# Attention, spatial gating and token mixing on one core: the order of all engines through the mixing stages comes from a list scheduler in the kernel

## The chip, the core and the metric

The kernel runs on one NeuronCore of a Trainium2 chip. Its engines work side by side, each through its own list of instructions in order: TensorE (PE, matrix products into PSUM), VectorE (DVE), ScalarE (ACT), GpSimd (POOL) and SyncE (SP), which here only issues transfers between DRAM and the on-chip memory. They wait for each other through semaphores. The metric is the device time of one execution in microseconds, the median of the runs shown; lower is better.

## The reference

Three computations follow one another; B = 4, H = 8 heads of D = 48, S = 768 positions, so that H x D = 384 columns.

```python
f = 1.0 / (1.0 + np.exp(-f_logit))
for t in range(S):                                   # gated linear attention
    state = f[:, :, t, :, None] * state + np.einsum('bhd,bhe->bhde', k[:, :, t], v[:, :, t])
    y[:, :, t] = np.einsum('bhd,bhde->bhe', q[:, :, t], state)
...
h = np.maximum(x @ w_in, 0.0)                        # spatial gating: d_ff = 1024
u, v = (h[..., :d_ff // 2], h[..., d_ff // 2:])
v_n = (v - mu) / np.sqrt(var + 1e-06)
v_s = np.einsum('ts,bsd->btd', w_spatial, v_n) + b_spatial[None, :, None]
x = (u * v_s) @ w_out
...
h = np.maximum(x.transpose(0, 2, 1) @ w_tok1, 0.0) @ w_tok2    # token mixing: 256
u = x + h.transpose(0, 2, 1)
return u + np.maximum(u @ w_ch1, 0.0) @ w_ch2                  # feed-forward: 1536
```

Most weights arrive as 64-bit floats, viewed as pairs of 32-bit words; w_spatial (w_sp) arrives as 32-bit floats.

## The kernel before

All products are made of a high and a low part (`mm3`: high x high, high x low, low x high), so every operand is first split: a rounded copy (high) and the rest (low).

**Attention.** The work is cut into 32 units: 4 batches x 2 halves of the sequence (384 positions) x 4 pairs of heads. A unit (`att_unit`, with `chunked`) loads fkq (keys, queries and decay logits of the pair), takes a sigmoid on ACT, two running products on VectorE (`tensor_tensor_scan`), scales keys and queries, then on TensorE transposes the keys and forms the pairs (`pt`, `pa`), on ACT copies them, on GpSimd masks them (`am`), on TensorE sums keys by values (`pk`), on VectorE carries the state from chunk to chunk, and on TensorE forms `py`, the sum of what the state and the masked pairs give. ACT and VectorE take the high and the low part of `py` into the tile x of that half. The fourth pair does not fit in its place: six small transfers scatter its rows over the other pairs' tiles. PSUM holds one `pt`, one `pk`, one `py` and one set of `pa`; there are three fkq buffers.

**Mixing stages.** For each batch and half, `s1` makes three `norm` tiles (nine products of 512 columns, Relu, mean and variance, scaled, split into vh and vl) and four `gate` tiles (nine products of 384 columns, Relu). `s23` makes four `mix` tiles for each half (18 products over all six tiles of vh and vl of the batch and the split w_sp; the bias added, times the gate, split again) and three `out1` tiles (twelve products with w_out; to DRAM as x1d). Their PSUM tiles come from a pool of three. A batch is 28 such tiles.

**Weights.** `split_weight` loads a piece of 384 columns into a staging buffer (`wst`, three of them, for 64-bit weights; `wsa`, three, for what is rounded). For 64-bit weights `rounded` makes a 32-bit float of the two words: two VectorE passes, an ACT scaling, a GpSimd addition. An ACT copy gives the high part; the low part is the difference, made for w_in, w_sp and w_out by two products on TensorE (the piece times the identity, minus the high part) and an ACT eviction. w_t1, w_t2 and w_c1 are rounded early, in 22 pieces, and stored to DRAM; they are loaded and split again in the last mixing stage, with a GpSimd subtraction.

**What sets the order.** The beginning, up to the first half's attention units, is written in a fixed turn (`apart`, `weave`) and then ordered by the framework's scheduler. From there on TensorE's order is as written: `run` walks through the mixing tiles and at set places (`turns`, counted in tiles) lets `keys` and `sums` take an attention unit one step further. The order of VectorE, ACT, GpSimd and SyncE is chosen by the framework's scheduler by its own model of the costs. `more` ties each early rounding piece to a gate or a mix by a small GpSimd operation (`pace`) on that tile. After the mixing stages comes the feed-forward (`ff`), whose order the change leaves as it is. A second body of the kernel (`general`), for inputs whose decay gets too small, is skipped here.

## Time and profile before

| | us |
|---|---|
| median of 3 runs (lowest, highest) | 797.63 (797.34, 800.44) |
| the profiled execution, its own time | 802.19 |
| its span, from the first to the last instruction | 800.5 |
| busy in the span: PE / DVE / ACT / POOL | 756.9 / 406.6 / 269.9 / 370.8 |

The profile is of one execution. PE busy is the time in which some product is in flight; products overlap in the pipeline, so a busy PE is not yet a full one. The granted clock is the share of TensorE's full speed that the chip allowed it. SyncE's own issuing and waiting are shown as SPq.

### The profile page before, as it was taken

Reading aid. Unit: us, or ns where it says so; the run is one execution under the profiler, and the core shown is the slowest. Engines: PE = TensorE matmul, PEld = TensorE weight load, DVE = VectorE, ACT = ScalarE, POOL = GpSimd, SP = SyncE. Lnnn points to the kernel's source line nnn. Section 1 sums busy time; section 2 is a strip of 40 time slices with the busy share of each in tenths; the row PEclk is TensorE's granted clock in tenths of the full one; section 3 lists DMA queues with packets and bytes.
Section 4 is the critical chain, followed back from the end, with each engine's and each line's share of the span. In section 5 each row is a group of like instructions: output and inputs, shape, how many; then the busy total and the mean of one; then the engine's idle time right before and its main releaser. Section 6 shows DMA issues by size and latency. Waiting matters only on the chain.

```text
span 800.5 us, 12918 instructions
## 1 busy us (share of the span) xinstructions
PE 756.9 (95%) x4860; PEld 709.4 (89%) x4860; DVE 406.6 (51%) x776; ACT 269.9 (34%) x602; POOL 370.8 (46%) x556
## 2 busy tenths in 40 slices
PE   5789999999989699999899999999999999999996
PEld 3557889988988589989899899999999999999996
DVE  6868776676887856862663862221222212221222
ACT  5556542344432444334523531121111211111110
POOL 4423421054532434222840898449546593448320
PEclk9989999999999699999999999999999999999999
DMA  8654422244564455302531623123131332104111
GB/s 266 198 177 137 129 73 75 89 124 129 169 193 150 129 180 169 78 38 74 159 99 57 185 85 115 54 86 95 54 93 39 129 90 80 49 18 123 44 44 35
DMA packets 48296, 86.33 MB, mean 108 GB/s; under 512 B 5472, under 2 KB 37344, under 8 KB 48224
## 3 DMA queue, kind: packets, MB, share of 16 engines
q1 hardware_dynamic: 48224, 85.42, 34.6%
q8 instruction: 40, 0.66, 0.4%
q14 instruction: 32, 0.26, 0.1%
HBM read 69.66 MB, written 13.37 MB: 104 GB/s over the span
## 4 chain that ended last, share of the span: by engine, by line
PE 72%; DVE 8%; DMA 8%; POOL 4%; issue 4%; ACT 3%; SPq 1%; DVEq 0%; POOLq 0%; ACTq 0%
PE po L744 18%; PE p L197 8%; PE p L196 8%; PE p L195 8%; DMA fkq<-in_fkq 4%; PE ps L195 3%; PE ps L197 3%; PE ps L196 3%; PE pa L292 2%; PE py L338 2%; PE py L346 2%; PE px L195 2%; PE px L196 2%; PE px L197 2%; PE pu L195 1%
## 5 line engine op out<-in xcount | busy, mean ns | idle before, releaser
L732 DVE SCALAR_TENSOR_TENSOR hl<-p,hh 128x384 fp32r<-128x384 f32 x96 | 53.2, 556 | 176.0 <-ACT hh L731 165.1
L731 ACT ACTIVATE hh<-p 128x384 fp32r<-128x384 f32 x96 | 47.1, 492 | 187.4 <-PE p L197 187.4
L744 PE MATMUL po<-hl,wc2h 128*128 128x384 f32 x288 | 97.5, 338 | 2.3 <-DVE hl L732 2.3
L744 PE MATMUL po<-hh,wc2l 128*128 128x384 f32 x288 | 96.7, 336 | 0.0
L744 PE MATMUL po<-hh,wc2h 128*128 128x384 f32 x288 | 75.0, 336 | 0.0
L195 PE MATMUL ps<-wsph,vh 128*128 128x384 f32 x192 | 66.5, 346 | 1.8 <-ACT vh L493 1.3
L131 POOL TENSOR_SCALAR look<-look 128x192 f32<-128x192 f32 x88 | 63.7, 724 | 7.6
L197 PE MATMUL ps<-wsph,vl 128*128 128x384 f32 x192 | 65.1, 339 | 0.7 <-DVE vl L494 0.7
L197 PE MATMUL p<-uh,wc1l 128*128 128x384 f32 x192 | 65.0, 338 | 0.0
L196 PE MATMUL ps<-wspl,vh 128*128 128x384 f32 x192 | 64.8, 338 | 0.0
L196 PE MATMUL p<-ul,wc1h 128*128 128x384 f32 x192 | 64.7, 337 | 0.0
L195 PE MATMUL p<-uh,wc1h 128*128 128x384 f32 x192 | 64.3, 338 | 0.0
L130 POOL TENSOR_TENSOR look<-look 128x192 f32<-128x192 f32 x88 | 45.7, 521 | 38.7 <-DMA look<-in_w_c 25.5
L297 POOL TENSOR_SCALAR_AFFINE_SELECT am<-am 128x384 f32<-128x384 f32 x64 | 44.2, 707 | 38.0 <-ACT am L296 37.7
L272 POOL COPY pend<-pg 128x3 f32<-128x3 f32 x32 | 10.7, 335 | 107.7 <-DVE pg L269 100.5
L755 POOL TENSOR_TENSOR us<-uh,ul 128x384 f32<-128x384 f32 x24 | 24.5, 1030 | 70.3 <-DVE ul L715 60.8
L744 PEld LDWEIGHTS po<-hl,wc2h 128*128 128x128 f32 x288 | 54.1, 188 | 3.3 <-DVE hl L732 3.3
L132 POOL TENSOR_TENSOR lows<-lows,look 128x192 f32<-128x192 f32 x88 | 53.4, 607 | 6.2
L744 PEld LDWEIGHTS po<-hh,wc2l 128*128 128x128 f32 x288 | 54.1, 188 | 0.0
L744 PEld LDWEIGHTS po<-hh,wc2h 128*128 128x128 f32 x288 | 52.3, 188 | 0.0
L269 DVE TENSOR_TENSOR_SCAN pg<-fs,first 128x384 f32<-128x384 f32 x32 | 31.2, 976 | 30.0 <-ACT first L406 29.6
L195 PEld LDWEIGHTS ps<-wsph,vh 128*128 128x128 f32 x192 | 36.6, 190 | 4.7 <-ACT vh L493 1.6
(332 smaller groups left out, 1972.3 us busy)
## 6 DMA issues: line engine op xcount, KB each, us to landing
fkq<-in_fkq SPq DMA_DIRECT2D x31, 578.0 KB, 4.2
look<-in_w_c SPq DMA_DIRECT2D x48, 192.0 KB, 2.4
vt<-in_v SPq DMA_DIRECT2D x8, 576.0 KB, 5.2
x1d<-xs SPq DMA_DIRECT2D x24, 192.0 KB, 1.9
xf<-x1d SPq DMA_DIRECT2D x12, 384.0 KB, 4.5
out<-ot SPq DMA_DIRECT2D x24, 192.0 KB, 2.4
look<-in_w_in SPq DMA_DIRECT2D x16, 192.0 KB, 3.1
look<-in_w_t SPq DMA_DIRECT2D x16, 192.0 KB, 2.4
```

Of the source, the lines that this page charges most:

```text
L130: nc.gpsimd.tensor_tensor(out=hi, in0=hi, in1=hi, op=ALU.mult)
L131: nc.gpsimd.tensor_scalar(out=hi, in0=hi, scalar1=NEAR**2, scalar2=None, op0=ALU.is_lt)
L132: nc.gpsimd.tensor_tensor(out=to, in0=to, in1=hi, op=ALU.add)
L195: nc.tensor.matmul(ps, lh, rh, start=first and i == 0, stop=False, **kw)
L196: nc.tensor.matmul(ps, lh, rl, start=False, stop=False, **kw)
L197: nc.tensor.matmul(ps, ll, rh, start=False, stop=i == n - 1, **kw)
L269: nc.vector.tensor_tensor_scan(out=pc, data0=fs[:, :W], data1=first, initial=0.0, op0=ALU.mult, op1=ALU.add)
L297: nc.gpsimd.affine_select(out=am[j], in_=am[j], compare_op=ALU.is_ge, fill=0.0, base=0, pattern=[[0, NCW], [1, C]], channel_multiplier=-1,)
L731: nc.scalar.activation(hh, ps, AF.Relu)
L732: nc.vector.scalar_tensor_tensor(out=hl, in0=ps, scalar=0.0, in1=f32(hh), op0=ALU.max, op1=ALU.subtract)
L744: nc.tensor.matmul(po[c], l[:, ft, csl], r, start=ft == 0 and x == 0, stop=ft == NF - 1 and x == 2)
L755: nc.gpsimd.tensor_tensor(out=us[c], in0=f32(uh[:, c, tsl]), in1=f32(ul[:, c, tsl]), op=ALU.add)
```

## The change

1. A list scheduler, `settle`, runs in the kernel's own Python. Every step of the attention units, the mixing tiles and the weight pieces is a task with an engine, a cost in us, a rank, the tasks that it needs, and the buffers that it takes (a ring: how many there are, and which tasks give one back). It keeps a clock for each engine and one for the transfers. At each turn it takes, among the tasks that could start within 0.15 us of the soonest, the one of the lowest rank, and emits its instructions. TensorE, VectorE, ACT, GpSimd and SyncE then all run in the order in which the tasks were emitted.
2. The low parts of w_sp and w_out are made by a GpSimd subtraction; those of w_in still by TensorE. w_in comes in twelve pieces of 256 columns in place of nine, and the first six are loaded into a tile of their own (`room`, in the buffer of vl).
3. The units of a half begin with the fourth pair. The fourth unit's fkq uses a buffer of the gates (tag u). In later batches a unit's keys are summed in one TensorE task with the sums of the unit before.
4. `more` and its `pace` operations go. The early rounding pieces are tasks of their own.

The functions `keys`, `sums`, `apart`, `run` and `also` go, and `att_unit`, `s1` and `s23` are cut into the tasks of `att_tasks`, `s1_tasks`, `mix_tasks` and `out_tasks`, with the same operations. The core of the diff:

```diff
+    def split_weight(pool, stage, src, name, n, cols, eng, first=0, order=None, psum=None, tiny=False, step=WST, sts=()):
...
+        where = [(i, c0, min(step, cols - c0)) for i in range(n) for c0 in range(0, cols, step)]
+        where = order(where) if order else where
+        return h, l, [partial(piece, *x, *sts[n : n + 1]) for n, x in enumerate(where)]
...
+        units = [(b, hf, p) for b in range(B) for hf in range(2) for p in (NP - 1, *range(NP - 1))]
...
+                if k == NP - 1:
+                    fkq = up.tile([P, NJ, W], F32, tag="u", name=f"fkq{u}").rearrange("p j t -> p (j t)")[:, :FKQ]
+                else:
+                    fkq = at3.tile([P, FKQ], F32, tag="fkq", name=f"fkq{u}")
...
+        lag = 0.12
+        ended, clock, rings, dmas = {}, {}, {}, [0.0]
...
+        def settle(tasks):
+
+            users, unmet, ready = {}, {}, []
+            for t in tasks:
+                missing = {x for x in t["needs"] if x not in ended}
+                unmet[t["name"]] = len(missing)
+                for x in missing:
+                    users.setdefault(x, []).append(t)
+                if not missing:
+                    ready.append(t)
+
+            def start(t):
+                at = max([clock.get(t["eng"], 0.0)] + [ended[x] + lag for x in t["needs"]])
+                for tag, n, _ in t["rings"]:
+                    held = rings.setdefault(tag, [])
+                    if len(held) >= n:
+                        if any(x not in ended for x in held[-n]):
+                            return None
+                        at = max([at] + [ended[x] + lag for x in held[-n]])
+                return at
+
+            left_over = len(tasks)
+            while left_over:
+                at = [(start(t), t) for t in ready]
+                at = [x for x in at if x[0] is not None]
+                assert at, (left_over, [t["name"] for t in ready][:20], [n for n, c in unmet.items() if c][:20])
+                soon = min(x[0] for x in at)
+                when, t = min((x for x in at if x[0] <= soon + 0.15), key=lambda x: x[1]["rank"])
+                ready.remove(t)
+                left_over -= 1
+                for tag, _, release in t["rings"]:
+                    rings[tag].append(release)
+                t["fn"]()
+                clock[t["eng"]] = when + t["cost"]
+                done = when + t["cost"]
+                if t["eng"] == "SP":
+                    dmas[0] = done = max(dmas[0], done + 1.3) + t["kb"] / 270.0
+                    done += 0.9
+                for x in t["gives"]:
+                    ended[x] = done
+                    for y in users.pop(x, ()):
+                        unmet[y["name"]] -= 1
+                        if not unmet[y["name"]]:
+                            ready.append(y)
+
+        tasks = []
+
+        def task(name, eng, cost, rank, fn, needs=(), rings=(), kb=0.0, gives=()):
+            tasks.append(
+                dict(name=name, eng=eng, cost=cost, rank=rank, fn=fn, needs=[x for x in needs if x], rings=rings, kb=kb,
+                     gives=(name, *gives))
+            )
...
+                f"L{k}", "SP", 0.45 if k else 1.35, at - 7, f["load"], kb=592,
+                rings=[("u", 2, [f"SU{k}"]) if k == NP - 1 else ("fkq", 3, [f"SU{k}"])],
...
+                task(f"G{k}", "ACT", 0.65, at - 3.2, f["gate"], [f"L{k}", back1("SC")], [("fs", 2, [f"BK{k}"])])
+                task(f"SC{k}", "DVE", 1.15, at - 3, f["ahead"], [f"G{k}", back1("BK")], [("pg", 2, [f"MU{k}", f"PE{k}"])])
+                task(f"PE{k}", "POOL", 0.2, at - 2.8, f["ends"], [f"SC{k}"])
+                task(f"BK{k}", "DVE", 0.97, at - 2.5, f["back"], [f"SC{k}"])
+                task(f"MU{k}", "DVE", 1.0, at - 1.5, f["scale"], [f"BK{k}"])
+                task(
+                    f"A{k}", "PE", 1.1, at, f["turn"], [f"MU{k}", back1("A")], [("pt", 1, [f"KN{k}"]), ("pa", 1, [f"AM0{k}", f"AM1{k}"])]
+                )
...
+                past = [f"ST{k}", back1("FR")]
+                sums = [f"AF0{k}", f"AF1{k}", vt]
...
+                        f"J{k}", "PE", 1.9, at + 1.75, joint,
+                        [f"ST{k - 1}", f"AF0{k - 1}", f"AF1{k - 1}", f"KN{k}", f"V{(k - 1) // NP}", vt],
+                        [("py", 1, [f"YL{k - 1}"]), ("pk", 1, [f"ST{k}"])], gives=[f"PK{k}", f"FR{k - 1}", f"SU{k - 1}"],
...
+                    f"ST{k}", "DVE", 1.35, at + 1.9, f["state"],
+                    [f"PK{k}", f"PE{k}", back1("FR"), f"ST{k - NP}" if hf else None],
...
+        def piece_tasks(name, gen, rank, width, kind, ring=True):
+
+            g = gen()
+            r = width / 384
+            step = lambda: next(g, None)
+            if kind == "narrow":
+                task(f"{name}d", "SP", 0.45, rank, step, kb=192 * r, rings=[("wsa", 3, [f"{name}l"])])
+                task(f"{name}h", "ACT", 0.45 * r, rank + 2, step, [f"{name}d"])
+                task(f"{name}l", "POOL", 1.05 * r, rank + 2, step, [f"{name}h"])
+                return
+            ended_by = f"{name}h" if general and kind != "store" else f"{name}s" if general else f"{name}p"
+            task(f"{name}d", "SP", 0.4, rank - 2, step, kb=384 * r, rings=[("wst", 3, [ended_by])] if ring else [])
+            last_use = {"pe": f"{name}t", "pool": f"{name}l", "store": f"{name}s"}[kind]
+            task(f"{name}a", "DVE", 0.08 + 0.87 * r, rank, step, [f"{name}d"], [("wsa", 3, [last_use])])
+            task(f"{name}o", "ACT", 0.45 * r + 0.05, rank, step, [f"{name}d", f"{name}a"])
+            task(f"{name}p", "POOL", 1.5 * r, rank, step, [f"{name}o", f"{name}a"])
+            if kind == "store":
+                task(f"{name}s", "SP", 0.4, rank + 2, step, [f"{name}p"], kb=192 * r)
+                return
+            task(f"{name}h", "ACT", 0.45 * r, rank + 1, step, [f"{name}p"])
+            if kind == "pe":
+                task(f"{name}t", "PE", 1.0 * r, rank + 1, step, [f"{name}h"], [("m", 3, [f"{name}l"])])
+                task(f"{name}l", "ACT", 0.42 * r, rank + 1, step, [f"{name}t"])
+            else:
+                task(f"{name}l", "POOL", 1.05 * r, rank + 1, step, [f"{name}h"])
...
+                    f"P{n}", "PE", 2.07, t, product, x_ready + [f"win{x}l" for x in range(2 * NK)] * (b + hf == 0),
+                    [("m", 3, [f"RE{n}"])],
+                )
+                task(f"RE{n}", "ACT", 0.55, t - 2, relu, [f"P{n}"], [("r", 2, [f"VF{n}"])])
+                task(f"BN{n}", "DVE", 0.85, t - 1, stats, [f"RE{n}"], [("sm", 4, [f"VF{n}"])])
+                task(f"RS{n}", "POOL", 0.85, t - 3, root, [f"BN{n}"])
+                task(f"VF{n}", "DVE", 0.55, t - 1, full, [f"RS{n}"], [("vf", 2, [f"VL{n}"])])
+                task(
...
+                f"P{b}m{hf}{j}", "PE", 3.13, t, product,
+                [f"VL{b}{x}{y}" for x in range(2) for y in range(NCW)]
+                + [f"wsp{hf * NCH + x}l" for x in range(NCH)] * (b == 0) + [f"O{b}0{NCW - 1}"] * (hf == 1 and j > 1),
+                [("m", 3, [f"AD{n}"])],
+            )
...
+        room = vnp.tile([P, NCH, DH], U32, tag="vl", name="room")
+        room = room.rearrange("p n (c t) -> p n c t", t=2)
         winh, winl, steps = split_weight(
-            wr, wst, w_in, "win", NK, DFF, nc.tensor, order=lambda x: sorted(x, key=lambda y: -y[1]), psum=ps_m,
-            tiny=general,
+            wr, wst, w_in, "win", NK, DFF, nc.tensor, psum=ps_m, tiny=general, step=256,
+            order=lambda x: sorted(x, key=lambda y: (y[1] < DH, y[1])), sts=[room[:, n] for n in range(NCH)],
         )
-        weave(apart(range(NP)), staged(steps))
...
-        wsph, wspl, st_a = split_weight(wl, wst, w_sp, "wsp", NCH, S, nc.tensor, psum=ps_m)
-        wouth, woutl, st_b = split_weight(wl, wst, w_out, "wout", NJ, DM, nc.tensor, psum=ps_m, tiny=general)
-        ordered = ExitStack()
-        ordered.enter_context(tc.manual_schedule(engines={mybir.EngineType.PE}))
...
+        wsph, wspl, st_a = split_weight(
+            wl, wst, w_sp, "wsp", NCH, S, nc.gpsimd, order=lambda x: sorted(x, key=lambda y: y[1])
+        )
+        wouth, woutl, st_b = split_weight(wl, wst, w_out, "wout", NJ, DM, nc.gpsimd, tiny=general)
+        later = []
...
+        period = 4 * NJ + 4 * NCW
+        at = [-40, -36, -32, -28, -9, -7, -5, -3] + [
+            period * (k // (2 * NP) - 1) - 3.5 + (k % (2 * NP)) * period / (2 * NP) for k in range(2 * NP, len(units))
+        ]
+        for k, x in enumerate(at):
+            att_tasks(k, x)
+        for n, x in enumerate(steps):
+            piece_tasks(f"win{n}", x, -30 + n / 2 if n < NCH else -11 + n / 2, 256, "pe", n >= NCH)
+        task("bb", "SP", 0.5, 0, lambda: nc.sync.dma_start(out=bb, in_=b_sp.unsqueeze(0).to_broadcast([P, S])), kb=400)
+        for n, x in enumerate(st_a):
+            piece_tasks(f"wsp{n}", x, -4 + n * 0.7, WST, "narrow")
+        for n, x in enumerate(st_b):
+            piece_tasks(f"wout{n}", x, 2 + n, WST, "pool")
+        for n, x in enumerate(later):
+            piece_tasks(f"later{n}", x, 14 + 2.2 * n, WST, "store")
+        place = -7
...
-        def more(b, col):
-
-            if b and early:
-                pace["scale"] = scale = smp.tile([P, 1], F32, tag="pace", name=f"pace{len(early)}")
-                nc.gpsimd.tensor_scalar(
-                    out=scale, in0=col, scalar1=0.0, scalar2=2.0**-29, op0=ALU.mult, op1=ALU.add
-                )
-                early.pop(0)()
-                del pace["scale"]
```

## Rows read from the trace of the kernel before

**Rows 1.** Stages of the span: busy time of each engine, granted clock, transfers.
```profile
core 0: us, PE busy (x) PEld busy (x) DVE busy (x) ACT busy (x) POOL busy (x), PEclk, DMA share, GB/s
0.00:20.00 20.00, 10.21 (x55) 7.78 (x55) 13.11 (x24) 11.03 (x26) 8.29 (x26) 1.00 0.80 266
0.00:58.40 58.40, 40.09 (x287) 28.43 (x288) 42.27 (x82) 33.11 (x82) 23.16 (x46) 0.91 0.68 217
58.40:112.50 54.10, 51.75 (x376) 42.05 (x375) 43.58 (x91) 31.50 (x76) 21.84 (x34) 1.00 0.40 118
112.50:220.00 107.50, 106.51 (x818) 97.67 (x817) 74.94 (x160) 42.59 (x100) 33.37 (x58) 1.00 0.37 115
220.00:282.00 62.00, 51.42 (x337) 45.81 (x337) 48.44 (x92) 22.03 (x53) 21.55 (x34) 0.86 0.52 165
282.00:380.00 98.00, 98.00 (x715) 89.98 (x712) 58.59 (x126) 42.03 (x95) 31.25 (x54) 1.00 0.34 102
380.00:400.00 20.00, 17.28 (x87) 16.12 (x86) 13.13 (x15) 11.80 (x24) 17.93 (x17) 0.91 0.52 164
400.00:443.00 43.00, 43.00 (x253) 42.78 (x252) 20.83 (x35) 13.13 (x28) 13.10 (x13) 1.00 0.23 74
480.00:795.00 315.00, 314.18 (x1812) 313.19 (x1810) 74.89 (x141) 57.97 (x115) 175.42 (x271) 1.00 0.23 71
112.59:115.72 3.13, 3.13 (x20) 3.13 (x20) 0.06 (x1) 0.49 (x1) 0.00 (x0) 1.00 0.00 0
```
**Rows 2.** PE in order of time, 58 to 67 us: start, duration, instruction.
```profile
58.48 0.39 PE L195 MATMUL pv<-winh,x 128*128 128x512 f32 x1
...
60.53 0.82 PE L338 MATMUL py<-fkq,state 112*112 112x128 f32 x6
...
62.32 0.91 PE L163 MATMUL wsppl<-wspsa,ident 128*128 128x384 f32 x2
...
63.24 0.40 PE L195 MATMUL pv<-winh,x 128*128 128x512 f32 x1
...
65.30 0.36 PE L283 MATMUL pt<-ident,fkq 112*128 112x112 f32 x2
...
66.46 0.91 PE L163 MATMUL wsppl<-wspsa,ident 128*128 128x384 f32 x2
```
**Rows 3.** SyncE's waits, 0 to 60 us: total us, times, longest.
```profile
SPq L64 <- POOL winsa L77: 19.5, 9, 4.3
```
**Rows 4.** The chain that ended last, 0 to 60 us: start, duration, what.
```profile
22.49 7.08 DMA fkq<-in_fkq
```
**Rows 5.** PE's waits, 220 to 285 us: total us, times, longest.
```profile
PE py L338 <- DVE x L417: 6.9, 1, 6.9
```
**Rows 6.** Groups of POOL's instructions, 0 to 400 us: busy us, mean ns.
```profile
L159 POOL TENSOR_TENSOR wt2l<-wt2sa,wt2h 128x384 fp32r<-128x384 f32 x4 | 4.2, 1056 | 0.2
```
**Rows 7.** Groups of DVE's instructions, 0 to 120 us: busy us, mean ns, idle before.
```profile
L277 DVE TENSOR_TENSOR fkq<-fkq,pg 128x768 f32<-128x768 f32 x13 | 14.0, 1079 | 0.3
L269 DVE TENSOR_TENSOR_SCAN pg<-fs,first 128x384 f32<-128x384 f32 x13 | 12.4, 954 | 11.5 <-ACT first L406 11.4
L274 DVE TENSOR_TENSOR_SCAN pg<-fs,last 128x384 f32<-128x384 f32 x13 | 12.4, 952 | 0.2
L316 DVE SCALAR_TENSOR_TENSOR state<-z,pend,own 112x96 f32<-112x96 f32 x29 | 11.4, 394 | 4.1 <-PE py L338 3.5
L329 DVE SCALAR_TENSOR_TENSOR z<-z,pend,pk 112x48 f32<-112x48 f32 x24 | 6.1, 255 | 0.1
...
L481 DVE BATCH_NORM_STATS2 bs<-r 128x6 f32<-128x512 f32 x6 | 4.1, 682 | 0.0
```
**Rows 8.** DVE and POOL in order of time, 20 to 23 us: start, duration, instruction.
```profile
20.38 0.56 DVE L72 SCALAR_TENSOR_TENSOR winsa<-win0384st,winsa 128x384 uint32<-128x384 uint32 x1
...
21.24 1.26 DVE L72 SCALAR_TENSOR_TENSOR winsa<-win1384st,winsa 128x384 uint32<-128x384 uint32 x1
...
21.07 1.01 POOL L77 TENSOR_TENSOR winsa<-winsa,win0384st 128x384 uint32<-128x384 uint32 x1 [1.81 <-PE py L338]
```

More of the change, by code (lines that the diff above doesn't have):

```diff
@@ L66, in rounded @@
         )
-        yield
+        yield True
+        a = stage.tile([P, WST], U32, tag="wsa", name=f"{name}sa")[:, :width]
         lo, hi = st[:, :width, 0], st[:, :width, 1]
@@ L97, in piece @@
         def piece(i, c0, width):
-            at = stage.tile([P, WST], U32, tag="wsa", name=f"{name}da{i}{c0}")
-            a = yield from rounded(stage, at[:, :width], srcr[i], c0, width, f"{name}d{i}{c0}", tiny)
+            a = yield from rounded(stage, srcr[i], c0, width, f"{name}d{i}{c0}", tiny)
             nc.sync.dma_start(out=dst[i * P : (i + 1) * P, c0 : c0 + width], in_=a)
@@ L611, in body @@
+        tasks.clear()
         right.close()
```

630 lines of the change are left out of this document (367 added, 263 removed).

## The prediction

> **What bounds the kernel now.** I read the table of stages first. The last long stage, the feed-forward from 480 us on, keeps TensorE busy for 314.18 of 315.00 us at full clock, so nothing that orders the mixing stages can shorten it; the change can only work before 443 us. There the stages differ [rows 1]. From 282 to 380 us TensorE is busy for 98.00 of 98.00 us while seven attention units, norms, gates and mixes pass through: the interleaving as such costs nothing when it is ordered well. Time is lost in three places: before 58.4 us (40.09 busy), from 220 to 282 us (51.42 of 62.00, and a granted clock of 0.86), and from 380 to 400 us (17.28 of 20.00, clock 0.91).
>
> Busy time hides the fill of the pipeline, so I compare with what the work needs. A mix of 18 products of 384 columns takes 3.13 us, 0.174 each [rows 1]. A norm of nine 512-column products takes from 63.24 to 65.30, 2.06 us; an attention unit takes 1.16 us for its transposes and pairs (65.30 to 66.46) and 1.79 us for its keys and sums (60.53 to 62.32); the products of one w_sp residual take from 62.32 to 63.24, 0.92 us [rows 2]. The first mix starts at 112.6. Up to there were done: 6 norms (12.4), 8 gates of nine products (12.5), 9 residuals of w_in (about 7.5 at full clock, an estimate from their widths), 16 of w_sp and w_out (14.7), and about 11 units (32): 79 us of work, so 33.5 us are lost before the first mix. From 112.5 to 443 the visible losses are 1.0 us (to 220), 10.6 idle and 0.14 x 62 = 8.7 of half clock (to 282), 2.7 and 1.8 (to 400): 24.8 us, 19.3 of them in one stretch.
>
> Then I asked what ended the waits. In the first stretch SyncE stood 19.5 us in nine waits for staging buffers that GpSimd had to release [rows 3], and the chain shows what stood behind it: the fourth unit's fkq is issued at 22.49 and needs 7.08 us [rows 4]. In the bad stretch one wait of 6.9 us, for the VectorE subtraction that frees the PSUM tile py, is the whole story [rows 5]: TensorE's written order met VectorE in another order, full of rounding of w_c1. After it the clock was at the lower of its two levels (1.2 of 2.4 GHz) for part of the stretch, which doubled the damage.
>
> **The change, part by part.**
>
> *Residuals of w_sp and w_out leave TensorE.* Twelve and four pieces at 0.92 us: 14.7 us of TensorE removed [rows 2]. Each costs one GpSimd subtraction, 1.06 us by the same operation on w_t2 [rows 6], 17 us in all, and saves an ACT eviction. GpSimd was busy for 23.2 and 21.8 us in the first two stages [rows 1], so 17 more fit into 112 us. Some of these products fell into idle time before 58 us; that is inside the 33.5 us of loss and I don't take it twice. Gain 14.7.
>
> *Start.* Six w_in pieces (now 256 columns wide, twelve instead of nine) get staging of their own, the fourth unit's fkq gets a spare u buffer, and the fourth pair, whose rows are scattered by six transfers, goes first, so that its transfers are no longer last before the norm. SyncE's 19.5 us of standing and the 7.08 us of fkq behind it go. What is late next is VectorE and the staging buffers: the scheduler takes the task that can start soonest, so w_sp loads, issued when SyncE is free, take the three wsa buffers before w_in's pieces, which then queue behind w_sp's subtractions. Ahead of and with these stand four fkq (0.59 MB each by their shape), two v, nine w_in (0.26), three w_sp (0.2) and b_sp (0.4): 6.9 MB, 26 us at the 266 GB/s of the first 20 us [rows 1]. Six pieces at about 1 us of GpSimd, with masks between them, give a first norm near 42 us instead of 58.5 [rows 2].
>
> The second half of the first norm needs eight units. A unit costs VectorE 1.08 + 0.95 + 0.95 us for the product and two scans, and some 2.3 for states and the low part (the state rows alone are 11.4 + 6.1 us for about ten units) [rows 7]: 5.3. Eight units (42), twelve w_in pieces at 0.7 (8.5), three norms at three passes of 0.68 or so (6.3) make 57 us. VectorE ran at 72% and 81% in the first two stages [rows 1]; at 85% these take 67 us. Add some 6 us from the last product to the finished x (2.95 of TensorE and as much for copies and mask, an estimate) and 12.5 us of norms and gates: the first mix at about 86 instead of 112.6. By then 59 us of work are done (9 units, 24.9 of norms and gates, 7.5 of w_in), so 27 us are lost instead of 33.5: gain 6.5. With VectorE at 95% the first mix is at 79 and the gain 13; at 72% it is at 98 and the gain is -5.
>
> *All engines in one order.* The wait of 6.9 us and the half clock after it come from two orders that disagree; now one list gives both, with task costs near what the rows show (mix 3.13, norm 2.07, product of keys 1.0). The rounding of w_t1, w_t2 and w_c1 is no longer tied to gates by 26 small GpSimd operations but fills in where its engines are free. Of the 24.8 us I let 8 stay, because landing times and GpSimd's durations vary and every engine now waits in order: whatever stands behind a late task on VectorE, ACT, GpSimd or SyncE waits with it, and TensorE three PSUM tiles later. Gain 17; bounds 25 (all gone, as from 282 to 380) and 5 (only one of the stretches mended by a quarter).
>
> *No cost taken:* more instructions for narrower w_in pieces (under 1 us on VectorE, inside the 57); six scattered transfers split differently in time on SyncE, which loses its long waits; the joint TensorE step, whose products are the same. The tail from 443 us is unchanged.
>
> Sum: 14.7 + 6.5 + 17 = 38. The profiled execution took 802.19 us (span 800.5), 4.6 more than the median 797.63. It would become 764; the median 797.63 - 38 gives **760 us**.
>
> **A rule against it.** VectorE's second pass over a rounding piece takes 0.56 us alone at 20.38 and 1.26 at 21.24, while GpSimd's addition runs from 21.07 for 1.01 us [rows 8]: they get in each other's way. Sixteen added subtractions of 1.06 us could so hold VectorE for up to 17 us before the first mix, where it is nearly the bound.
> The Trainium skill, page "SBUF — State Buffer", section "Who interferes with whom", says that a VectorE instruction with two SBUF inputs and a GpSimd instruction that reads SBUF exclude each other for the whole instruction. The trace agrees in that pair, 0.56 against 1.26 us.
>
> **Rivals.**
> 1. *VectorE is held up by the added subtractions*: 57 + 17 = 74 us at 85% is 87, the first mix at 106, loss 47, 13 worse than before. 14.7 - 13 + 17 = 19: 779 us. For it: the pair of rows 8. Against: scans and evictions fill most of VectorE, and rows 7 give the second scan the same 0.95 us although GpSimd was at work for two fifths of those 112 us. Chance 0.10.
> 2. *The stall moves*: the planner's landings and GpSimd costs are off, and another 20 us are lost after the first mix: 14.7 + 0 + 5 = 20, 778 us. Against: its costs equal the rows. Chance 0.15.
> 3. *Slower: TensorE meets each unit too early.* A written order on five engines has no slack for a late VectorE state; TensorE stands at each unit's sums as it did once for 6.9 us. Some 23 units follow the first mix; at 38 / 23 = 1.65 us each the whole gain is gone, at 2.5 us it is 57 - 38 = 19 lost: 817 us. For it: the 6.9 us show what one such meeting costs. Against: TensorE's order was already written by hand and lost nothing in 98 us for seven units. Chance 0.08.
> 4. *The change does not do what it says*: the list comes out as nearly the old order, and the residuals' 14.7 us are eaten by a start in which w_in waits for w_sp: 797 us. Chance 0.05.
>
> **How the numbers follow.** The forecast, 0.62, gives 760, with a range of its own from 745 (14.7 + 13 + 25 = 53 gained) to 783 (14.7 - 5 + 5). Rivals 1 and 2 lie inside it at 779 and 778. The range to give 8 in 10 reaches some 7 us below, for idle time that the busy figures hide, and a few above: 738 to 787. Faster by over 0.5%, about what a measurement of this kernel can tell from no change: 0.62 + 0.10 + 0.15 = 0.87; within it 0.05; slower 0.08.
>
> **What would show it.** Right: no residual product of w_sp or w_out on TensorE; the first norm before 50 us and the first mix between 79 and 98; no single TensorE wait over 3 us after the first mix and a granted clock of 1.00 from there on; the feed-forward as long as before; VectorE over 80% up to the first mix. Wrong: the first mix after 100 us with VectorE full (rival 1); waits of 1 to 3 us before most units' sums (rival 3); the feed-forward itself longer, because w_t1, w_t2 or w_c1 arrive late, which I have priced at nothing.

## The result and the profile after

The changed kernel takes **788.06 us** (786.48 to 789.71, 4 runs) where the kernel before takes 797.49 (796.79 to 800.44) beside it: ratio 0.9875, 95% interval 0.9842 to 0.9908. It is faster by 9.4 us; 38 were forecast, and 788 lies just outside the range. The profiled execution took 788.79 us, its span is 787.1.

The stages, same columns as [rows 1], with the first norm at 64.65 and the first mix at 115.72:

```profile
core 0: us, PE busy (x) PEld busy (x) DVE busy (x) ACT busy (x) POOL busy (x), PEclk, DMA share, GB/s
0.00:64.60 64.60, 44.00 (x310) 32.98 (x310) 44.77 (x84) 28.92 (x73) 28.80 (x53) 0.98 0.59 193
64.60:115.70 51.10, 43.97 (x271) 37.29 (x269) 43.74 (x80) 28.37 (x71) 32.00 (x41) 0.89 0.44 135
0.00:115.70 115.70, 87.97 (x579) 70.28 (x579) 88.51 (x164) 57.29 (x144) 60.80 (x93) 0.94 0.52 167
115.80:240.00 124.20, 121.27 (x934) 111.44 (x935) 108.88 (x216) 54.67 (x134) 48.95 (x66) 1.00 0.56 178
240.00:360.00 120.00, 119.96 (x920) 109.62 (x919) 84.47 (x175) 46.78 (x110) 28.05 (x50) 1.00 0.24 72
466.00:781.00 315.00, 314.49 (x1813) 313.50 (x1812) 74.56 (x141) 57.75 (x115) 175.39 (x271) 1.00 0.23 71
```

PE in order of time, the first product of the first norm, the first of the second half's norms, and the first of the first mix (start, duration, instruction):

```profile
64.65 0.80 PE L191 MATMUL pv<-winh,x 128*128 128x512 f32 x1
...
100.06 0.79 PE L191 MATMUL pv<-winh,x 128*128 128x512 f32 x1
...
115.72 0.44 PE L191 MATMUL ps<-wsph,vh 128*128 128x384 f32 x1
```

Two halves come out. From the first mix to the end of the span it is now 787.1 - 115.7 = 671.4 us, where it was 800.5 - 112.6 = 687.9: 16.5 gained. TensorE is busy for 121.27 of 124.20 and 119.96 of 120.00 us at full clock, and the stretch that had clock 0.86 [rows 1] and the wait of 6.9 us [rows 5] is gone. PE's longest waits between the first mix and the feed-forward are now these (total us, times, longest):

```profile
PE po L998 <- DVE hl L986: 2.3, 2, 1.5
PE pt L349 <- issue: 1.6, 1, 1.6
```

Before the first mix it went the other way: 115.7 us instead of 112.6, with TensorE busy for 3.9 us less in them (87.97 against 40.09 + 51.75 in [rows 1]). TensorE thus stood idle for 27.7 us there, 7.0 more than before. VectorE was busy for 88.51 us against 85.85 before (42.27 + 43.58), GpSimd for 60.80 against 45.00. PE's waits up to the first mix have many small heads and one large:

```profile
PE pt L349 <- DVE fkq L344: 8.6, 3, 7.8
PE py L417 <- DVE x L443: 3.9, 2, 2.0
PE py L417 <- DVE state L393: 3.8, 4, 1.1
PE winpl L158 <- POOL win20sa L78: 3.6, 1, 3.6
PE winpl L158 <- POOL win1512sa L78: 2.4, 1, 2.4
```

What fed those waits shows in SyncE's queue. It issued w_sp's loads (L149) among w_in's, and stood for their buffers, the third group for 12.43 us (start, duration, issue):

```profile
14.33 1.89 SPq L149 DMA_DIRECT2D wspsa<-in_w_sp  x3
...
31.09 4.47 SPq L149 DMA_DIRECT2D wspsa<-in_w_sp  x2
...
40.53 12.43 SPq L149 DMA_DIRECT2D wspsa<-in_w_sp  x3
```

SyncE's waits up to 64.6 us (total, times, longest) answer to [rows 3]: the 19.5 us of standing are still there, under other names: 11.7 behind the GpSimd subtraction that was added, and 7.6 behind TensorE's products for w_in.

```profile
SPq L149 <- POOL wspl L154: 11.7, 3, 7.7
SPq L149 <- PE winpl L158: 7.6, 3, 3.8
```

VectorE's groups up to the first mix answer to [rows 7]: the first scan went from 954 to 1019 ns, the second from 952 to 1029, the state row from 394 to 520. The product with the keys went the other way, from 1079 to 980. The added GpSimd group is the last row.

```profile
L393 DVE SCALAR_TENSOR_TENSOR state<-z,pend,own 112x96 f32<-112x96 f32 x24 | 12.5, 520 | 1.1
L329 DVE TENSOR_TENSOR_SCAN pg<-fs,first 128x384 f32<-128x384 f32 x12 | 12.2, 1019 | 6.6 <-ACT first L324 6.6
L338 DVE TENSOR_TENSOR_SCAN pg<-fs,last 128x384 f32<-128x384 f32 x11 | 11.3, 1029 | 0.2
L344 DVE TENSOR_TENSOR fkq<-fkq,pg 128x768 f32<-128x768 f32 x11 | 10.8, 980 | 0.1
```
```profile
L154 POOL TENSOR_TENSOR wspl<-wspsa,wsph 128x384 fp32r<-128x384 f32 x12 | 12.5, 1047 | 8.0 <-ACT wsph L151 8.0
```

So my theory after the result, still to be tested: what failed lies before the first mix, where VectorE sets the end and GpSimd's work stretches VectorE's; TensorE's removed products were no part of that. The rivals: the start is late because w_sp's loads go before w_in's, or because the ninth unit (rank -3.5) is served before the eighth (rank -3), which the second half's norms need.

To compare kernels, one number serves below: TensorE's idle time ahead of the last 320.5 us of the span, which is the feed-forward in all of them. The names are those of the experiments below. The last column is the mean granted clock up to there, and the busy time holds the clock too: a norm's first product takes 0.80 us at 64.65 and 0.79 at 100.06 in the changed kernel, in a stretch with a clock of 0.89, and 0.39 at 58.48 in the kernel before [rows 2].

| kernel | until, us | TensorE busy | idle | clock |
|---|---|---|---|---|
| before | 480.0 | 442.71 | 37.3 | 0.97 |
| changed | 466.6 | 432.34 | 34.3 | 0.99 |
| changed, residuals on TensorE | 470.5 | 443.99 | 26.5 | 0.97 |
| mended start | 464.3 | 429.76 | 34.5 | 0.97 |
| mended, w_sp subtractions left out | 454.8 | 426.82 | 28.0 | 0.97 |
| mended, residuals on TensorE | 454.5 | 431.05 | 23.5 | 0.99 |
| the same, later fkq held | 453.9 | 433.82 | 20.1 | 1.00 |

### The profile page after: what moved, and what is told of

Its sections match the earlier page's. It is cut to its first block, busy times and chain, and to the rows that moved or that the text cites. A ratio compares the mean times of both kernels' runs of the same rounds, so it can differ in the third digit from the quotient of the medians.

```text
span 787.1 us, 12875 instructions
## 1 busy us (share of the span) xinstructions
PE 746.2 (95%) x4821; PEld 704.4 (89%) x4821; DVE 419.7 (53%) x783; ACT 262.3 (33%) x596; POOL 381.2 (48%) x549
## 4 chain that ended last, share of the span: by engine, by line
PE 81%; DVE 6%; DMA 4%; POOL 3%; issue 2%; ACT 2%; SPq 0%; DVEq 0%; POOLq 0%; ACTq 0%
PE po L998 18%; PE p L193 8%; PE p L192 8%; PE p L191 8%; PE pa L354 4%; PE ps L191 4%; PE ps L193 3%; PE ps L192 3%; PE py L426 3%; PE py L417 3%; PE px L191 2%; PE pu L191 2%; PE pv L191 2%; PE pu L193 2%; PE pu L192 2%
## 5 line engine op out<-in xcount | busy, mean ns | idle before, releaser
L369 POOL TENSOR_SCALAR_AFFINE_SELECT am<-am 128x384 f32<-128x384 f32 x64 | 43.9, 705 | 58.4 <-ACT am L365 58.2
L329 DVE TENSOR_TENSOR_SCAN pg<-fs,first 128x384 f32<-128x384 f32 x32 | 32.1, 1005 | 19.5 <-ACT first L324 19.5
L969 DVE TENSOR_TENSOR ul<-p,uh 128x384 fp32r<-128x384 f32 x24 | 13.3, 556 | 46.5 <-ACT uh L968 46.5
```

The lines of the kernel that those rows point to most:

```text
L329: nc.vector.tensor_tensor_scan(out=pc, data0=d["fs"][:, :W], data1=first, initial=0.0, op0=ALU.mult, op1=ALU.add)
L369: nc.gpsimd.affine_select(out=am, in_=am, compare_op=ALU.is_ge, fill=0.0, base=0, pattern=[[0, NCW], [1, C]], channel_multiplier=-1,)
```

## The experiments

**1. What the residuals on TensorE cost.** First the one part alone, in the kernel before:

```diff
-        wsph, wspl, st_a = split_weight(wl, wst, w_sp, "wsp", NCH, S, nc.tensor, psum=ps_m)
-        wouth, woutl, st_b = split_weight(wl, wst, w_out, "wout", NJ, DM, nc.tensor, psum=ps_m, tiny=general)
+        wsph, wspl, st_a = split_weight(wl, wst, w_sp, "wsp", NCH, S, nc.gpsimd)
+        wouth, woutl, st_b = split_weight(wl, wst, w_out, "wout", NJ, DM, nc.gpsimd, tiny=general)
```

> The kernel before, with one part of the change alone: the low parts of w_sp and w_out by a GpSimd subtraction instead of two TensorE products. The term of the sum as forecast: 14.7 us less, 783. Rival: most of these products stood in time that TensorE would have waited anyway (before 112 us it waits for attention units), so 0 to 5 us less, 793 to 797. Third: GpSimd holds up VectorE, over 800.

Measured: 800.21 us, ratio 1.0037 (1.0019 to 1.0055). The term that was to bring 14.7 us costs 3. The first mix is at 115.14 instead of 112.59; up to it VectorE was busy for 90.21 us instead of 85.85, GpSimd for 65.57 instead of 45.00 (columns as above):

```profile
56.40:115.00 58.60, 47.48 (x342) 39.92 (x339) 46.95 (x91) 26.41 (x63) 33.60 (x42) 0.85 0.34 106
0.00:115.00 115.00, 87.19 (x613) 68.81 (x614) 90.21 (x172) 58.59 (x141) 65.57 (x94) 0.85 0.52 165
```

The first line shows where the removed products went. From the first norm, here at 56.49, to the first mix TensorE is busy for 47.48 of 58.60 us at a clock of 0.85. In the kernel before it was busy for 51.75 of 54.10 at 1.00 there [rows 1]. In that stretch it now waits 10.4 us, in two waits, for the VectorE subtraction that frees py, against 0.6 before.

Then that part alone undone in the changed kernel ("narrow pe" and "pe" put the low part's task on TensorE and ACT):

```diff
-            wl, wst, w_sp, "wsp", NCH, S, nc.gpsimd, order=lambda x: sorted(x, key=lambda y: y[1])
+            wl, wst, w_sp, "wsp", NCH, S, nc.tensor, psum=ps_m, order=lambda x: sorted(x, key=lambda y: y[1])
...
-        wouth, woutl, st_b = split_weight(wl, wst, w_out, "wout", NJ, DM, nc.gpsimd, tiny=general)
+        wouth, woutl, st_b = split_weight(wl, wst, w_out, "wout", NJ, DM, nc.tensor, psum=ps_m, tiny=general)
...
-            piece_tasks(f"wsp{n}", x, -4 + n * 0.7, WST, "narrow")
+            piece_tasks(f"wsp{n}", x, -4 + n * 0.7, WST, "narrow pe")
...
-            piece_tasks(f"wout{n}", x, 2 + n, WST, "pool")
+            piece_tasks(f"wout{n}", x, 2 + n, WST, "pe")
```

> The changed kernel with one part undone: the low parts of w_sp and w_out are made by products on TensorE again. If VectorE sets the end up to the first mix and GpSimd's subtractions only stretch it, the sixteen products fall into TensorE's idle time there: the first mix at 111 to 115 us (115.7 with the subtractions) and a time of 782 to 788 us. If the 14.7 us of products count as the prediction has it, the time is 788 + 14.7 = 803 us, and something else ate the start.

Measured: 790.87 us, ratio 0.9902 (0.9864 to 0.994), against 0.9875 with the subtractions; the intervals overlap. It is not the 803 of the one theory, and not quite the 782 to 788 of the other: the removal is worth 0.0027 x 797.5 = 2.2 us, which can't be told from nothing; first mix 118.83 against 115.72. By the table, the removal lets TensorE's busy time fall by 443.99 - 432.34 = 11.7 us and its idle time rise by 7.8. The place of the first mix was a miss: 111 to 115 was expected with VectorE freed, and it came 3.1 us later although VectorE is busy for 84.0 us up to it instead of 88.5. In this start, then, VectorE's work alone does not set the end.

**2. The two faults of the start, mended.** One: w_sp's loads wait for the sixth w_in piece's VectorE passes. Two: ranks of the fifth to eighth units. Each alone, then both.

```diff
-            piece_tasks(f"wsp{n}", x, -4 + n * 0.7, WST, "narrow")
+            piece_tasks(f"wsp{n}", x, -4 + n * 0.7, WST, "narrow", behind=[f"win{2 * NK - 1}a"])
...
-        at = [-40, -36, -32, -28, -9, -7, -5, -3] + [
+        at = [-40, -36, -32, -28, -20, -18, -16, -14] + [
```

> The changed kernel, with one need added: no w_sp load is issued before the sixth w_in piece has its staging buffer. Theory A (staging: the w_sp loads hold the three wsa buffers and w_in's pieces queue behind them): the first norm falls from 64.6 us to 40 to 48, the first mix from 115.7 by about 10, the time to about 778. Theory B (the fourth unit of the second half is the late one, because unit 8 gets its fkq buffer first): the first norm falls just the same, but the first mix stays within 3 us of 115.7 and the time at 785 to 789. Theory C (VectorE's work alone bounds the start): the first mix stays, and VectorE is over 85% busy up to it.

Measured: 786.54 us, ratio 0.9869 (0.984 to 0.9898), no different from the change. The first norm comes at 40.57 instead of 64.65, near the 42 of the prediction, and the first mix at 114.65 instead of 115.72. All but one of the 24 us are given back before the first mix: w_sp's loads were a fault, but not what set the end.

> The changed kernel, with other ranks for units 4 to 7 alone (-20, -18, -16, -14 instead of -9, -7, -5, -3), so that unit 7 goes before units 8 and 9 for its fkq buffer and on every engine. Theory A (staging): nothing that matters moves, 786 to 789. Theory B: the second half's first norm moves from 100.5 us to about 90 and the first mix from 115.7 to 105 to 110; 779 to 783. Theory C (VectorE bound): the order of equal work changes little, 785 to 789.

Measured: 784.9 us, ratio 0.9834 (0.9804 to 0.9863); first norm 62.94, the first of the second half's norms 84.46 instead of 100.06, first mix 108.51. The first mix is where theory B had it, the time is not (779 to 783), and its interval overlaps that of the change.

> Both edits together: w_sp behind w_in, and the new ranks for units 4 to 7. If A and B each hold a part of the start: first norm at 40 to 48, first mix at 98 to 106, 772 to 779. If B alone: as with the ranks alone, 779 to 783. If C (VectorE bound): 784 to 789, VectorE over 85% busy up to the first mix.

Measured: 783.79 us, ratio 0.9823 (0.9795 to 0.9851); first norm 39.49, first mix 107.00; the interval still overlaps that of the change a little. Its stages:

```profile
39.50:85.00 45.50, 33.13 (x238) 25.96 (x237) 42.32 (x71) 24.52 (x63) 29.34 (x40) 0.85 0.51 154
...
0.00:107.00 107.00, 81.67 (x607) 66.17 (x608) 90.14 (x165) 58.58 (x148) 60.58 (x94) 0.94 0.56 179
```

With the loads out of the way VectorE is busy for 42.32 of 45.50 us (93%) while TensorE is for 33.13. By this VectorE looks like the bound of the mended start, which still needs 90 us of VectorE for a first mix; the next experiment tests it.

**3. How much of that is GpSimd's doing.** The mended start with w_sp's twelve subtractions left out: an ACT copy stands in their place, so that its low part is not the difference.

```diff
             if eng is not nc.tensor:
+                if eng is nc.scalar:
+                    nc.scalar.copy(l[sl], a)
+                    return
...
-            wl, wst, w_sp, "wsp", NCH, S, nc.gpsimd, order=lambda x: sorted(x, key=lambda y: y[1])
+            wl, wst, w_sp, "wsp", NCH, S, nc.scalar, order=lambda x: sorted(x, key=lambda y: y[1])
```

> The mended start with GpSimd's twelve subtractions for w_sp left out: an ACT copy of the piece stands in their place, so the low part of w_sp is not the difference, and part of the computation is changed. TensorE has none of these products either. If the subtractions hold up VectorE by their own length (12 x 1.06 = 12.7 us): VectorE's scans between 40 and 85 us come back from 1.4-1.8 towards 0.95 us, the first mix comes at 95 to 100, 772 to 777 us. If VectorE has simply that much work and the subtractions cost it little: scans stay long, first mix at 105 to 108, 782 to 786 us.

Measured: 776.83 us, ratio 0.9743 (0.9711 to 0.9774), 6.4 us under the mended start (0.9823 - 0.9743 = 0.0080); first mix 101.87. The two theories' windows were 95 to 100 and 105 to 108; it fell between them, so the subtractions hold VectorE up, but by less than their own length. VectorE makes the same 165 instructions up to the first mix, in 83.07 us here against 90.14 with the subtractions. That is 7.1 us for 12 subtractions, 0.59 each if all of it is theirs. It is the instructions that get shorter, not waits for GpSimd: VectorE's idle time up to the first mix is 107.00 - 90.14 = 16.9 us in the mended start and 101.80 - 83.07 = 18.7 here. Nor is it the clock, which is lower here, 0.90 against 0.94, while the first mix comes 5.1 us earlier. The first scan in the mended start, then the stages and the scan here:

```profile
L329 DVE TENSOR_TENSOR_SCAN pg<-fs,first 128x384 f32<-128x384 f32 x12 | 13.8, 1147 | 5.7 <-ACT first L324 5.7
```
```profile
0.00:101.80 101.80, 81.62 (x607) 66.55 (x608) 83.07 (x165) 63.12 (x160) 48.63 (x82) 0.90 0.57 187
```
```profile
L332 DVE TENSOR_TENSOR_SCAN pg<-fs,first 128x384 f32<-128x384 f32 x12 | 11.4, 951 | 6.4 <-ACT first L327 6.4
```

The disputed cost by itself, two engines and nothing else (`meet` lets both start together, `less` is GpSimd's subtraction, N is 12):

```python
    steps = [
        ("scan_alone", scan, None), ("product_alone", product, None), ("two_alone", two_in, None), ("one_alone", one_in, None),
        ("none", None, less), ("scan", scan, less), ("product", product, less), ("two", two_in, less), ("one", one_in, less),
    ]
    for n, (name, dve, gps) in enumerate(steps):
...
        meet(n)
...
        for _ in range(N):
            if dve:
                dve(dt)
            if gps:
                gps(pt)
```

> The disputed cost by itself: no attention and no mixing, the output is filled with zeros. VectorE makes twelve of each of four instructions alone (the scan and a subtraction of two 128x384 inputs, the product of two 128x768 inputs, a one-input pass of 128x384), GpSimd twelve subtractions of 128x384 alone, then each VectorE series runs beside GpSimd's subtractions. If the two engines hold each other up, the 0.95 us scan and the 1.06 us subtraction take up to 2.0 us each when side by side, and the one-input pass is stretched less. If the long scans of the changed kernel have another cause (transfers, semaphores), side by side they keep their durations within 10%.

Measured, by groups of instructions ("alone" and "none" are without the neighbour):

```profile
L57 POOL TENSOR_TENSOR p_product<-full,one 128x384 f32<-128x384 f32 x12 | 18.6, 1549 | 0.9
L45 DVE TENSOR_TENSOR d_product<-wide 128x768 f32<-128x768 f32 x12 | 18.2, 1519 | 0.4
L57 POOL TENSOR_TENSOR p_scan<-full,one 128x384 f32<-128x384 f32 x12 | 17.9, 1495 | 0.9
L42 DVE TENSOR_TENSOR_SCAN d_scan<-fs,one 128x384 f32<-128x384 f32 x12 | 17.6, 1464 | 0.4
L57 POOL TENSOR_TENSOR p_two<-full,one 128x384 f32<-128x384 f32 x12 | 14.2, 1183 | 0.9
L48 DVE TENSOR_TENSOR d_two<-full,one 128x384 f32<-128x384 f32 x12 | 13.4, 1119 | 0.4
L57 POOL TENSOR_TENSOR p_one<-full,one 128x384 f32<-128x384 f32 x12 | 12.1, 1005 | 0.9
L57 POOL TENSOR_TENSOR p_none<-full,one 128x384 f32<-128x384 f32 x12 | 11.9, 992 | 0.9
L45 DVE TENSOR_TENSOR d_product_alone<-wide 128x768 f32<-128x768 f32 x12 | 11.5, 958 | 0.4
L42 DVE TENSOR_TENSOR_SCAN d_scan_alone<-fs,one 128x384 f32<-128x384 f32 x12 | 11.5, 957 | 0.4
L51 DVE TENSOR_SCALAR d_one<-words 128x384 uint32<-128x384 uint32 x12 | 11.1, 925 | 0.4
L48 DVE TENSOR_TENSOR d_two_alone<-full,one 128x384 f32<-128x384 f32 x12 | 6.7, 558 | 0.4
L51 DVE TENSOR_SCALAR d_one_alone<-words 128x384 uint32<-128x384 uint32 x12 | 4.3, 361 | 0.4
```

Beside a subtraction the scan takes 1464 ns instead of 957, the product 1519 instead of 958, and GpSimd's subtraction itself about 1.5 us instead of 0.99. VectorE's own two-input subtraction goes from 558 to 1119, GpSimd's beside it to 1183. So in these means one subtraction costs VectorE 0.51 to 0.56 us. They hold the first of each twelve, which began ahead of GpSimd and was not stretched; the middle values are 1566, 1632, 1232 and 1038 ns for scan, product, two inputs and one, 0.61 to 0.68 more than alone. The 0.59 in the kernel lies between. The expectation for the one-input pass was wrong: it is stretched most for its length, from 361 to 925 ns, while GpSimd keeps its 1.0 us.

The Trainium skill, page "SBUF — State Buffer", section "Who interferes with whom", calls the shared ports an exclusive lock held for the whole instruction. The direction agrees; the size does not quite: one after the other a scan and a subtraction would take 957 + 992 = 1949 ns, and side by side, by the middle values, the scan takes 1566 and the subtraction 1522.

**4. The mended start with the residuals on TensorE.** The edits of experiments 1 (the second) and 2 together, and one of the gates' needs:

```diff
-                    x_ready + [f"win{2 * NK + x + NK * (j // 2)}l" for x in range(NK)] * (b + hf == 0), [("m", 3, [f"RU{n}"])],
+                    x_ready + [f"win{2 * NK + x + NK * (j // 2)}l" for x in range(NK)] * (b == 0), [("m", 3, [f"RU{n}"])],
```

> The mended start (w_sp loads behind w_in, units 5 to 8 ranked ahead of the rest, 783.8 us, first mix at 107) with the low parts of w_sp and w_out on TensorE. If VectorE is the bound there and GpSimd stretches its instructions: first mix at 100 to 106, 776 to 783 us. If TensorE's products count: 783.8 + 14.7 = 798 us, first mix at 107 or later.

Measured: 779.41 us, ratio 0.9774 (0.9741 to 0.9808), against 0.9823 without these products: here adding TensorE's work back wins 0.0049 x 797.5 = 3.9 us (the intervals overlap a little). The first mix is at 88.66, earlier than expected, with two w_in pieces, four of w_sp's and all of w_out's behind it; so the place of the first mix alone is no fair measure, and the table's idle time is: 23.5 us instead of 34.5. From the first norm to the first mix TensorE is now nearly full, and at full clock, where the mended start had 33.13 of 45.50 us at 0.85:

```profile
37.95:88.60 50.65, 47.04 (x359) 36.89 (x358) 43.98 (x93) 30.61 (x77) 18.17 (x36) 1.00 0.42 135
```

How much of the 3.9 us comes from the clock and how much from VectorE without the subtractions was not separated here.

On top of it, the loads of the ninth and later units held:

```diff
-                f"L{k}", "SP", 0.45 if k else 1.35, at - 7, f["load"], kb=592,
+                f"L{k}", "SP", 0.45 if k else 1.35, at - 7, f["load"], ["A7"] if k >= 2 * NP and not general else (), kb=592,
```

> The mended start with the low parts of w_sp and w_out on TensorE (779.4 us), and the loads of the ninth and later units held until the eighth's pairs are on TensorE, so that VectorE gets nothing of later units before the first mix. If VectorE's work ahead of the first mix is the bound, three or four units of about 5 us go behind it and TensorE's idle time before the feed-forward (23.5 us) falls by 3 to 8 us: 772 to 777. If that work only moves to where VectorE is needed next, no change: 778 to 782, with TensorE's idle time after the first mix longer by what is saved before it.

Measured: 776.84 us, ratio 0.9751 (0.9723 to 0.9778), first mix 91.86, idle time 20.1 us. The intervals overlap with the kernel above, so a gain from holding these loads is not shown. Of the kernels that leave nothing out it is the fastest: 797.17 - 776.84 = 20.3 us under the kernel before.

**5. Whose order is it?** The 16.5 us after the first mix were put down to one order for all engines. Here only TensorE keeps the list's order, and the framework's scheduler orders the rest:

```diff
-                engines={
-                    mybir.EngineType.PE, mybir.EngineType.DVE, mybir.EngineType.Activation, mybir.EngineType.Pool,
-                    mybir.EngineType.SP,
-                }
+                engines={mybir.EngineType.PE}
```

> The changed kernel, but only TensorE runs in the list's order; VectorE, ACT, GpSimd and SyncE get theirs from the framework's scheduler as before. If the 16.5 us won after the first mix come from TensorE and VectorE following one list, most of it is lost: single TensorE waits over 3 us and half-clock stretches after the first mix are back, 795 to 810 us. If the new list for TensorE alone (joint keys and sums, no ties of roundings to gates) does it, the time from the first mix to the end stays at 671 us and the kernel at 785 to 790 us.

Measured: 807.63 us, ratio 1.0126 (1.0093 to 1.0159), slower than the kernel before. First mix at 125.08, 12.5 us later than in the kernel before. PE's longest waits ahead of the feed-forward are for VectorE again, and larger:

```profile
PE py L417 <- DVE state L393: 14.5, 6, 5.0
PE py L417 <- DVE x L443: 8.9, 3, 5.0
```

But all of the first and 6.6 us of the second lie before the first mix. Behind it the longest is another:

```profile
PE pk L378 <- ACT kn L361: 4.2, 1, 4.2
```

From the first mix to the end the span takes 807.0 - 125.1 = 681.9 us, against 687.9 before the change and 671.4 with it. So of the 16.5 us some 6 are left with TensorE's list alone. Of the 19.9 us between this span and the changed kernel's, 9.4 lie ahead of the first mix and 10.5 behind it.

The same with VectorE in the list's order as well:

```diff
-                engines={mybir.EngineType.PE}
+                engines={mybir.EngineType.PE, mybir.EngineType.DVE}
```

> The changed kernel with TensorE and VectorE in the list's order, ACT, GpSimd and SyncE in the framework scheduler's own. With TensorE alone in the list's order it took 1.0126 of the kernel before, with all five 0.9875. If the agreement of TensorE and VectorE is what counts: 788 to 793 us. If SyncE's and GpSimd's order count as much (loads issued late, masks behind roundings): 797 to 808 us.

Measured: 803.01 us, ratio 1.0072 (1.0046 to 1.0098); from the first mix to the end 801.2 - 116.7 = 684.5 us. My expectation that TensorE and VectorE are the pair that counts fell. Now VectorE waits in its order for engines in another. All engines from 173.6 to 179.6 us of its span: VectorE stands 1.67 us for ACT's late copy of py, so everything behind it is late, the scaling of the next unit's keys (L344) too, and TensorE has stood for 5.07 us when that is done:

```profile
174.61 0.46 ACT L439 CAST x<-py 112x384 fp32r<-112x384 f32 x1
...
175.10 0.56 DVE L443 TENSOR_TENSOR x<-py,x 112x384 fp32r<-112x384 f32 x1 [1.67 <-ACT x L439]
...
178.52 0.95 DVE L344 TENSOR_TENSOR fkq<-fkq,pg 128x768 f32<-128x768 f32 x1
...
179.57 0.61 PE L349 MATMUL pt<-ident,fkq 112*128 112x112 f32 x2 [5.07 <-issue]
```

And the changed kernel with all but SyncE in the list:

```diff
                     mybir.EngineType.PE, mybir.EngineType.DVE, mybir.EngineType.Activation, mybir.EngineType.Pool,
-                    mybir.EngineType.SP,
```

> The changed kernel with four engines in the list's order and only SyncE (the issue of transfers) in the framework scheduler's. With TensorE and VectorE alone in the list it took 1.0072 of the kernel before, with all five 0.9875, and its ACT stood 39.9 us in 24 waits for loads of fkq against 7.6 us in 5. If the late issue of loads is what costs: 798 to 806 us and the 24 waits stay. If ACT's and GpSimd's own order costs (copies of x late, masks behind roundings): 786 to 791 us.

Measured: 789.76 us, ratio 0.9909 (0.9881 to 0.9937); the interval overlaps that of the changed kernel. From the first mix to the end it takes 788.0 - 116.3 = 671.7 us. ACT's waits for fkq (total, times, longest) with four engines in the list:

```profile
ACT fs L322 <- DMA fkq<-in_fkq: 10.2, 5, 4.7
```

and with two, where they were the suspect:

```profile
ACT fs L322 <- DMA fkq<-in_fkq: 39.9, 24, 4.5
```

So the late loads followed from ACT's and GpSimd's orders, and SyncE's own order adds nothing that can be told. ACT's and GpSimd's places in the list are worth (1.0072 - 0.9909) x 797.5 = 13 us, and by the spans all of it lies behind the first mix (684.5 - 671.7 = 12.8).

## Why the prediction was wrong

*The residuals (14.7).* The first of the failed steps, and the larger: "14.7 us of TensorE removed ... Gain 14.7". It measured 2.2 us in the changed kernel (within the error of nothing), -2.9 in the kernel before and -3.9 in the mended start (there with one need of the gates changed beside it). The products did leave: no product of w_sp's or w_out's low part is on TensorE. But they all lay ahead of the first mix (w_sp's from 44.9 to 86.5 us of the trace before), and there TensorE depends on what VectorE hands it. It already stood idle for 20.7 us [rows 1], but 18.3 of these lie before 58.4 us, with four of w_sp's twelve pieces. The other eight, and w_out's four, stood where TensorE was full, 51.75 of 54.10 us, and they brought nothing either: taken out of the kernel before, they came back as 10.4 us of waits for VectorE's part of x and as a clock of 0.85 instead of 1.00 (experiment 1). I had counted the idle time as "inside the 33.5 us of loss" and subtracted nothing for it, and put the rest down as time won. The subtractions did not merely "fit into 112 us" of GpSimd: each costs VectorE over half a microsecond.

*Start (6.5).* The second, and it failed in the same place: together with the 14.7 it was to bring 21.2 us ahead of the first mix, and that stretch came out 3.1 us longer, the first mix at 115.7 instead of 86. The late w_in that the text names came worse than priced (first norm 64.65, not 42), but mending it moved the first norm by 24 us and the first mix by 1. The step that failed is "57 us" of VectorE, and with it the share of 85%. By the start of the second half's norms, at 100.06, VectorE had been busy for 75.30 us, 75% of the time: it had ten scans each way behind it, not eight, and all of w_out. Two of the later pieces follow before the first mix, up to which it was busy for 88.51 us. With 75.30 for 57 the prediction's own sum gives a first mix at 107 at 85%, and at 98 at 95%, not 86. VectorE was full only in places (13.64 of 14 us from 71 to 85, 42.32 of 45.50 in the mended start). Taking 7.1 us from it moved the first mix of the mended start by 5.1; in the start as changed, 4.5 us less of VectorE, with the products back on TensorE, moved nothing forward, and there the ranks hold the end too: with the second half's units ranked ahead, the first mix came at 108.51 (experiment 2). Part of the price is the clock: TensorE, waiting on VectorE, was granted 0.89 from 64.6 to 115.7 us, where it had 1.00 before [rows 1]; its products at 100 us take 0.79 and 0.63 us, and 0.39 from 103.4 on.

*One order for all engines (17).* Right in its mechanism: 16.5 us between the profiled executions, and the agreement brings the larger part. Behind the first mix 6.0 of them are left with TensorE's list alone, 3.4 with VectorE's too, and 16.2 with all but SyncE's. What those few us without agreement come from (the joint step, the missing `pace` operations, or the executions themselves) was not tested. TensorE's list alone loses 10 us in all, because it puts the first mix 12.5 us later. That 17 met 16.5 is partly luck, and the size is less sure than it looks: the profiled execution before is 4.6 us above its median, the one after 0.7, so some 4 of the 16.5 may be that execution's own. That reasoning holds for the sum too: 16.5 - 3.1 = 13.4 between the profiles, 9.4 between the medians. In what share the 4 belong to which stretch is left open.

*No cost taken.* Right for the feed-forward: 314.49 of 315.00 us busy, as before.

*Rival 1* named the mechanism and was given 0.10. Its place was right, VectorE ahead of the first mix, and so was its direction. Its price, 17 us for sixteen subtractions, was too high (0.51 to 0.68 us each, 8 to 11 in all), and it left the 14.7 us standing, which were the larger error. What was held against it, the scans' 0.95 us in [rows 7], was no evidence: of the 26 scans up to the first mix of the kernel before, only three ran beside one of GpSimd's two-input additions, and each of the three began ahead of it. There the scan kept its 0.95 us and the addition took 1.31 to 1.55:

```profile
12.73 0.94 DVE L274 TENSOR_TENSOR_SCAN pg<-fs,last 128x384 f32<-128x384 f32 x1
...
12.89 1.31 POOL L77 TENSOR_TENSOR winsa<-winsa,win1768st 128x256 uint32<-128x256 uint32 x1 [0.36 <-DVE winsa L72]
```

In [rows 8] GpSimd's addition began first, and VectorE's pass took 1.26.

*Rival 2*, the stall that moves, did not happen: no TensorE wait is over 1.6 us between the first mix and the feed-forward. *Rival 3* did not either in the changed kernel; with one engine in the list TensorE did meet the units too early, at 807.63 us, but ahead of the first mix and not at the 23 units behind it. *Rival 4* had the early fault right (w_in behind w_sp), not its weight.

Put together: between the profiled executions 13.4 us were won. Of what is missing to 38, the two terms ahead of the first mix make up 24.3 us (21.2 forecast, -3.1 measured, the residuals' 2.2 inside it), and the order behind it half a microsecond. The medians differ by 9.4 only, because the profiled execution before stood 4.6 us above its median and the one after 0.7.

## What to carry to other kernels

Before counting work taken off an engine as time, ask which engine hands it the next work in the stretch where the removed work lies, also where it looks full: here TensorE's busy time fell by 11.7 us, and its idle time rose by 7.8; in the kernel before its clock fell with it. Work given to GpSimd has a price on VectorE, some 0.6 us for a subtraction of 128x384 here, and it is to be asked for where VectorE is nearly full. A written order helps when every engine that takes part in the exchange follows the same one; TensorE's alone was slower than none.

## What was not expected of the hardware

A VectorE pass with one SBUF input (integer, every second word) went from 361 to 925 ns beside GpSimd's subtractions, more than the scan (957 to 1464), and GpSimd did not slow down (992 to 1005). With the scan and the product both engines slowed by about half, and VectorE's two-input subtraction took twice its time. In the kernels, where the two overlapped for long, the one that began second was stretched: in the changed one the scan that began at 77.34, ahead of an addition at 77.65, took 0.95 us, and the one at 69.40, behind an addition at 69.25, took 1.41. The Trainium skill, page "SBUF — State Buffer", section "Who interferes with whom", says that a VectorE instruction with one SBUF input contends only in its two-port modes, which such a pass can enter. Whether this one had, no run here shows.
